# A fused scan and feed-forward kernel: another order of SyncE's transfers in its first quarter

## The chip, the cores and the metric

The kernel runs on one core of one Trainium2 chip. The metric is the device time of one execution in microseconds (us); the lower, the better. A core has four engines that compute: TensorE (PE, matrix products; its weight loads are listed apart as PEld), VectorE (DVE), ScalarE (ACT) and GpSimd (POOL). SyncE (SP) computes nothing: in this kernel it issues nearly all transfers between memory and the core's buffers (DMA), one after another, in the order of the program.

## The reference, cut to what matters

A scan (`mamba2_ssd`, 4 batches, 8 heads, 768 tokens, head size 32, state size 16) makes `x` of 3072 tokens by 256; a feed-forward block with a quick GELU follows.

```python
# scan: a is a decay per token and head, B and C are the state's input and output
log_a = np.log(np.clip(a, 1e-06, 1.0))
for c in range(nc):                            # chunks of 32 tokens
    cum = np.cumsum(la, axis=-1)
    L = np.exp(cum[:, :, :, None] - cum[:, :, None, :]) * causal
    M = np.einsum('bhin,bhjn->bhij', Cc, Bc) * L
    y_intra = np.einsum('bhij,bhjd->bhid', M, xc)
    y_inter = np.einsum('bhin,bhnd->bhid', Cc, state) * np.exp(cum)[:, :, :, None]
    y[:, :, sl] = y_intra + y_inter
    state = decay_full * state + sum_j(Bc * xc * decay_from_j)   # written short
# feed-forward: x (3072, 256), w_in (256, 2048), w_out (2048, 256)
h = x @ w_in
g = h * (1.0 / (1.0 + np.exp(-1.702 * h)))
return (g @ w_out).astype(np.float32)
```

The two weight matrices arrive as 64-bit floats and are turned into 32-bit ones on the core.

## The kernel before

The tokens are worked off in six groups of 512. A group is two pairs; a pair is 256 tokens, two chunks of 128. Pairs 0 and 1 are group 0, pairs 2 and 3 group 1, pairs 4 and 5 group 2 (the third). While TensorE computes the feed-forward part of one group, the scan of the next group's pairs is put between its matmuls.

The weights come in ten pieces, 0 to 5 of w_in and 6 to 9 of w_out. A piece is fetched as raw 64-bit words into one of four buffers of the tag "bits", and VectorE and ScalarE turn it into floats in four steps; after the last of them (`join`) the buffer is free:

```python
    def words(name):
        return wide.tile([P, 2 * PN], U32, tag="bits", name=name, bufs=BUFS)   # BUFS = 4
    # fields(i): DVE L178, L181, the first readers of a fetched piece
    # clamp(i):  ACT L189, L190      rounded(i): DVE L194
    NEXT = {1: (6,), 4: (7,), 5: (8,), 7: (9,)}

    def join(i):
        ...                            # DVE L205, L211: the piece's floats to w_in or w_out
        for n in NEXT.get(i, ()):
            fetch(n)                   # SyncE L166: the next piece into a buffer that is free

    def narrow(i):
        rounded(i)
        if i + 1 < len(PIECES):
            fields(i + 1)
        join(i)
```

The decays `a` of later pairs reach the core by a detour: `store_a` clips them (VectorE L341) and stores them to a scratch tensor in memory, and `spread` reads them back, copied to all partitions, into a buffer of the same four. `decay` scans what was spread:

```python
    def spread(p):
        if p - 2 in ra:
            ra[p] = ra[p - 2]
        else:
            ra[p] = words(f"a{p}").bitcast(FP32)...        # cut
        for i, side in enumerate(SIDES):
            nc.sync.dma_start(out=ra[p][side], in_=scratch[...])     # SyncE L237, a<-scratch

    def decay(p):
        ...
        nc.vector.tensor_tensor_scan(out=L, data0=ra[p]..., data1=idents..., ...)   # DVE L388
        for k in range(2):
            ends(p, k)                                               # DVE L437
```

`load(p)` loads b, c and x of a pair (SyncE L140; for pairs from 4 on, `load_blocks` loads B and C in another layout, SyncE L124, and `load` adds b and x). `spread_rows(b)` loads the a of a whole batch in another layout (SyncE L246, af); `clip_rows` and `decay_rows` work on it (VectorE L447, L460). `turn(p)` transposes b and c of a pair on TensorE (tp, L554), copies them out (ACT L547) and makes CsT on VectorE (L612). `gain` is TensorE's A (L657), `score` its cb (L626), `finish` its y (L730, L742); `finish` is the last reader of the pair's x.

Group 0 runs as sixteen steps of `hidden(0, f)` (TensorE h, L783) and then sixteen of `project_all(0)` (TensorE o, L900), step f of which reads w_out's block f, so four steps use one piece. At its end VectorE (L906, ob) empties the two banks of o, and the third h of group 1 takes the bank that is emptied first. Work of the other engines is hung to these steps:

```python
    at(in_hidden[0], 5, store_a)
    at(in_hidden[0], 6, lambda: pick_a(PG))
    at(in_hidden[0], 9, lambda: fan_all(PG))
    at(in_hidden[0], 9, since_fanned)
    for i, k, c in ((2, 1, 1), (3, 2, 2), (4, 4, 4), (5, 6, 6), (6, 9, 12), (7, 12, 15)):
        at(in_hidden[0], k, lambda i=i: narrow(i))
        at(in_hidden[0], c, lambda i=i: clamp(i + 1))
    at(in_hidden[0], 5, lambda: spread(PG + 1))
    at(in_hidden[0], 6, lambda: load(PG + 1))                 # PG = 2
    n, p = 2 * PG, 3 * PG
    pairs = PG, PG + 1
    at(in_project[0], 0, lambda: turn(PG), lambda: narrow(8))
    at(in_project[0], 1, lambda: clamp(9))
    at(in_project[0], 2, lambda: decay(PG + 1), lambda: clip_rows(1),
       lambda: decay_rows(1), lambda: turn(PG + 1))
    at(in_project[0], 5, lambda: narrow(9))
    at(in_project[0], 9, lambda: gain(pairs), lambda: score(pairs), lambda: keep_both(pairs),
       lambda: weigh(PG), lambda: weigh(PG + 1))
    at(in_project[0], 13, lambda: finish(pairs))
    at(in_project[0], 14, lambda: mix_in(1), lambda: mix_in(2), lambda: mix_in(3),
       lambda: turn_blocks(2), lambda: mix_y(1), lambda: decay(n))
    for k in range(PG):
        at(in_project[0], 8 + k, lambda k=k: load(2 * PG + k))
    for k, i in enumerate((9, 13)):
        at(in_project[0], i, lambda k=k: spread(2 * PG + k))
```

Each engine keeps the order of the program, SyncE too: a transfer that waits for a buffer holds up those behind it. At the start `keep_busy` lets TensorE multiply ones while the first data are on their way.

Of the kernel before, what the change touches and what calls it, by code (L numbers as in the profile page):

```python
# [16 lines left out]
P = 128  # L17
# [18 lines left out]
def kernel(  # L36
# [31 lines left out]
    nc = tc.nc  # L68
# [16 lines left out]
    PG = CG // 2  # L85
    R = 4
    Q = NH // R
    H = P // 2
# [27 lines left out]
    def load_blocks(p, queues=(nc.sync, nc.sync)):  # L116

        g, n = divmod(p, PG)
        b, c = divmod(2 * p, NC)
        for queue, name, src in zip(queues, "CB", (C, B)):  # L120
            if n == 0:
                blocks[name, g] = raw.tile([P, 2, PG * P], FP32, tag="z", name=f"z{name}{g}", bufs=2)
            for r in range(R):
                queue.dma_start(  # L124
                    out=blocks[name, g][32 * r:32 * r + 32, :, n * P:(n + 1) * P],
                    in_=src[b, Q * r:Q * r + Q, c * P:(c + 2) * P].rearrange(
                        "q (i f) n -> i q (f n)", i=32))

    def load(p, parts=None):
        if parts is None:  # L130
            parts = "bcx" if p < 2 * PG else "bx"
            if p >= 2 * PG:
                load_blocks(p)
        for part in parts:
            dst, src, e = {"b": (rb, B, N), "c": (rc, C, N), "x": (rx, x, D)}[part]
            dst[p] = raw.tile([P, 2, NH, e], FP32, tag=part, name=f"{part}{p}", bufs=3)
            for k in range(2):
                b, c = divmod(2 * p + k, NC)
                sl = slice(c * P, (c + 1) * P)
                nc.sync.dma_start(out=dst[p][:, k], in_=src[b, :, sl, :].rearrange("h s d -> s h d"))  # L140
# [9 lines left out]
    def words(name):  # L150
        return wide.tile([P, 2 * PN], U32, tag="bits", name=name, bufs=BUFS)

    def fetch(i):
        name, f, n = PIECES[i]
        if n == 2 and f % 4:
            t = pieces.pop(i - 1)[:, 2 * n * DM:]
        else:
            t = pieces[i] = words(f"bits{i}")
            t = t[:, :2 * n * DM]
        if name == "in":  # L160
            src = moe_w_in[:, 2 * f * P:2 * (f + n) * P].rearrange("(k p) e -> p k e", p=P)
            dst = t.rearrange("p (k e) -> p k e", k=NK)
        else:
            src = moe_w_out[f * P:(f + n) * P, :].rearrange("(f p) e -> p f e", p=P)
            dst = t.rearrange("p (f e) -> p f e", f=n)
        nc.sync.dma_start(out=dst, in_=src)  # L166
        t = t.rearrange("p (e w) -> p e w", w=2)
        bits[i] = t[:, :, 0], t[:, :, 1]
# [5 lines left out]
    def fields(i):  # L174
        hi, cols = bits[i][1], slice(0, PIECES[i][2] * DM)
        mantissa[i] = wide.tile([P, PN], U32, tag="m", name=f"m{i}")[:, cols]
        power[i] = wide.tile([P, PN], U32, tag="p2", name=f"p2{i}")[:, cols]
        nc.vector.tensor_scalar(out=power[i], in0=hi, scalar1=0x7FF00000, scalar2=None,  # L178
                                op0=ALU.bitwise_and)

        nc.vector.tensor_scalar(out=mantissa[i], in0=hi, scalar1=0x000FFFFF,  # L181
                                scalar2=0x00100000, op0=ALU.bitwise_and, op1=ALU.bitwise_or)

    def clamp(i):


        e = power[i]
        z = e.bitcast(FP32)
        nc.scalar.activation(z, e, AF.Relu, scale=-8.0, bias=edge[:, 0:1])  # L189
        nc.scalar.activation(e, z, AF.Relu, scale=-1.0, bias=edge[:, 1:2])  # L190
# [5 lines left out]
                                       op0=ALU.mult, op1=ALU.add)  # L196


    NEXT = {1: (6,), 4: (7,), 5: (8,), 7: (9,)}

    def join(i):

# [6 lines left out]
        else:  # L209
# [4 lines left out]
            op0=ALU.mult, op1=ALU.mult)  # L214
        for n in NEXT.get(i, ()):
            fetch(n)
# [6 lines that stand above are left out]
# [5 lines left out]
# [5 lines that stand above are left out]
            ra[p] = words(f"a{p}").bitcast(FP32)[:, :2 * NH * H].rearrange(  # L233
                "p (k e) -> p k e", k=2)
        b, c = divmod(2 * p, NC)
        for i, side in enumerate(SIDES):
            nc.sync.dma_start(  # L237
                out=ra[p][side],
                in_=scratch[c:c + 2, i, b * NH:(b + 1) * NH].rearrange("c h i -> c (h i)").unsqueeze(
                    0).to_broadcast([H, 2, NH * H]))  # L240
# [3 lines left out]
    def spread_rows(b):  # L244
        raf[b] = raw.tile([P, NC, P], FP32, tag="af", name=f"af{b}", bufs=1)
        nc.sync.dma_start(out=raf[b].rearrange("p c s -> p (c s)"),  # L246
                          in_=a[b].unsqueeze(1).to_broadcast([NH, N, S]))
# [9 lines left out]
    for r in range(R):  # L257
        (nc.sync, nc.scalar)[r % 2].dma_start(
            out=az0[32 * r:32 * r + 32].rearrange("p k s -> p (k s)"),
# [26 lines left out]
    ones = const.tile([P, P], FP32, name="ones")  # L286
# [34 lines left out]
    def fold_ident(k):  # L321
# [12 lines left out]
        out=cum.rearrange("p k s -> p (k s)"), data0=carry.rearrange("p k s -> p (k s)"),  # L334
# [13 lines left out]
    def pick_a(p):  # L348

        b, c = divmod(2 * p, NC)  # L350
        X = ffn.tile([P, 2, DM], FP32, tag="ob", name=f"X{p}")
        X = fans[p] = X.rearrange("p k (q i) -> p k q i", q=Q)
        for q in range(Q):
            nc.scalar.activation(X[:, :, q], az[:, c:c + 2], AF.Copy, scale=pick[:, b, q:q + 1])
# [5 lines left out]
        out=same, in_=same, pattern=[[-N, NH], [0, D]], compare_op=ALU.is_ge,  # L360
        fill=0.0, base=0, channel_multiplier=1)
    nc.gpsimd.affine_select(
        out=same, in_=same, pattern=[[N, NH], [0, D]], compare_op=ALU.is_ge,
# [4 lines left out]
    for t, head in ((whose[:, 1:], PG), (whose[:, :1], 1)):  # L368
# [8 lines left out]
        out=part, in_=same[:, :, 0].rearrange("p (r q) -> p q r", q=Q), op=ALU.add, axis=AX.X)  # L377
# [36 lines left out]
    def keep_busy(n):  # L414

        t = bank("busy")
        for i in range(4 * n):
            nc.tensor.matmul(out=t[:, :P], lhsT=ones, rhs=ones,
                             start=True, stop=True, skip_group_check=True)

    def decay_heads(p, r, ab):
# [116 lines left out]
    def bank(name):  # L538
        return ps.tile([P, 4 * P], FP32, tag="ff", name=name)

    def area(name):
        return psa.tile([P, R, 4 * P], FP32, tag="cb", name=name)
# [34 lines left out]
    def turn_blocks(g):  # L577

        t = {}
        for name in "CB":  # L580
            t[name] = ssd.tile([P, TG], FP32, tag=f"{name}t", name=f"{name}t{g}", bufs=1)
            nc.vector.transpose(
                out=t[name].rearrange("p (n i f) -> p n f i", n=PG, i=32),
                in_=blocks.pop((name, g)).rearrange("p h (f n) -> p f h n", n=N))
        for n in range(PG):
            s = st[g * PG + n] = {}
            s["BT"], s["tp"] = (
                t[name][:, n * 2 * P:(n + 1) * 2 * P].rearrange("p (k i) -> p k i", k=2)
                for name in "BC")
# [240 lines left out]
    def mix_y(g):  # L830
        mixed_y[g] = ffn.tile([P, 4, HT], FP32, tag="my", name=f"my{g}", bufs=1)
        mix(mixed_y[g], yT[g].rearrange("p k (t e) -> p k t e", t=2))
# [231 lines left out]
    def differ_of(p, rs):  # L1064
        differ(p, [(r, ab[p, r]) for r in rs])

    keep_busy(2)
    ab0 = area("ab0")
    for r in range(R):
        ab[0, r] = ab0[:, r, :2 * Q * H]  # L1070
# [40 lines left out]
    finish((1,))  # L1111
    join(1)
    load(PG)
    spread_rows(1)
    fields(2)
    clamp(2)
    add_up(1, (3,))
# [2 lines left out]
    def at(places, i, *work):  # L1120
        places.setdefault(i, []).extend(work)

    in_hidden = [{} for _ in range(NG)]
    in_project = [{} for _ in range(NG)]
# [2 lines left out]
        for i, side in enumerate(SIDES):  # L1127
            nc.sync.dma_start(out=scratch[:, i].rearrange("c r i -> r c i"), in_=az[:32, :, side])

    at(in_hidden[0], 5, store_a)  # L1130
    at(in_hidden[0], 6, lambda: pick_a(PG))
    at(in_hidden[0], 9, lambda: fan_all(PG))
    at(in_hidden[0], 9, since_fanned)
    for i, k, c in ((2, 1, 1), (3, 2, 2), (4, 4, 4), (5, 6, 6), (6, 9, 12), (7, 12, 15)):
        at(in_hidden[0], k, lambda i=i: narrow(i))
        at(in_hidden[0], c, lambda i=i: clamp(i + 1))
    at(in_hidden[0], 5, lambda: spread(PG + 1))
    at(in_hidden[0], 6, lambda: load(PG + 1))
    n, p = 2 * PG, 3 * PG
    pairs = PG, PG + 1  # L1140
    at(in_project[0], 0, lambda: turn(PG), lambda: narrow(8))
# [6 lines left out]
    at(in_project[0], 13, lambda: finish(pairs))  # L1148
    at(in_project[0], 14, lambda: mix_in(1), lambda: mix_in(2), lambda: mix_in(3),
       lambda: turn_blocks(2), lambda: mix_y(1), lambda: decay(n))  # L1150
    for k in range(PG):
        at(in_project[0], 8 + k, lambda k=k: load(2 * PG + k))
    for k, i in enumerate((9, 13)):
        at(in_project[0], i, lambda k=k: spread(2 * PG + k))


    after = {}
# [83 lines left out]
    k = NF // 2 - 1  # L1241
# [6 lines left out]
    for g in range(2, NG):  # L1248
        n, p = (g + 1) * PG, (g + 2) * PG
# [52 lines left out]
        k = NF // 2 - 1  # L1302
# [42 lines left out]
```

## Time and profile before

The time before is 369.91 us, the median of three runs (367.86 to 371.13). The profiled execution has a span of 366.9 us.

| engine | busy us | share of the span |
|---|---|---|
| PE | 351.3 | 96% |
| PEld | 301.7 | 82% |
| DVE | 250.9 | 68% |
| ACT | 148.0 | 40% |
| POOL | 12.9 | 4% |

The page cuts the span into 40 equal slices of 9.17 us. PE and DVE are the busy tenths of a slice, PEclk the clock that TensorE was granted in tenths of full speed, DMA the busy share of the sixteen DMA engines (an overflow shows as 0), and GB/s what they moved:

```profile
PE   7889999799699999998999999999999999999996
...
DVE  5799966994776989694869384779393355274453
...
PEclk9899999899699999999999999999999999999999
DMA  5898697405486000066101525100010000010001
```

In the first eleven slices, some 100 us, lie nearly all the slices in which TensorE is less than 0.8 busy; there the weights are fetched and turned into floats. A wait in the profile is written as who waited for whom, and the chain of waits follows the work that ended last back through the program. SyncE's rows in the timeline (SPq) are the issues, not the movement of the data.

### The profile page before, as it was taken

The page shows a single profiled execution, that of the slowest core. Times are in us where ns is not written, and L with a number is a line of the kernel's source. Part 1 is how long each engine was busy: PE and PEld are TensorE (multiplying, and loading weights), DVE is VectorE, ACT ScalarE, POOL GpSimd, SP SyncE. Part 2 cuts the span into 40 slices and gives each one's busy share as a digit, 9 for nine tenths or more (in the row PEclk, how much of TensorE's full clock was granted, in tenths as well). Part 3 has the DMA queues.
Part 4 walks back from the last instruction along what each step waited for, and adds up shares of the span by engine and source line. Part 5 has one row for each costly group of instructions (what it writes and reads, how often), then busy time and mean ns, then how long its engine had stood idle before and what let it go on. Part 6 is the DMA issues. An engine that isn't in the chain of part 4 may idle for free.

```text
span 366.9 us, 9051 instructions
## 1 busy us (share of the span) xinstructions
PE 351.3 (96%) x3880; PEld 301.7 (82%) x3880; DVE 250.9 (68%) x479; ACT 148.0 (40%) x329; POOL 12.9 (4%) x40
## 2 busy tenths in 40 slices
PE   7889999799699999998999999999999999999996
PEld 6554468687279999987999989999989999989996
DVE  5799966994776989694869384779393355274453
ACT  4588564003143431553433364333354331453330
POOL 6310000100000010000000000000000000000000
PEclk9899999899699999999999999999999999999999
DMA  5898697405486000066101525100010000010001
GB/s 120 145 364 196 186 188 178 74 2 113 119 158 107 13 2 2 25 159 127 53 3 38 92 70 98 23 2 2 1 60 4 0 2 1 2 57 2 0 2 57
DMA packets 73055, 26.10 MB, mean 71 GB/s; under 512 B 58552, under 2 KB 66616, under 8 KB 73016
## 3 DMA queue, kind: packets, MB, share of 16 engines
q1 hardware_dynamic: 72184, 25.14, 30.3%
q8 instruction: 30, 0.49, 0.6%
q10 hardware_dynamic: 832, 0.39, 0.4%
q14 instruction: 9, 0.07, 0.1%
HBM read 22.28 MB, written 3.24 MB: 70 GB/s over the span
## 4 chain that ended last, share of the span: by engine, by line
PE 75%; DMA 11%; DVE 6%; SPq 5%; issue 2%; ACT 0%; POOL 0%; DVEq 0%; POOLq 0%
PE acc L964 34%; PE X L858 18%; PE Y L868 13%; DMA bits<-in_moe_w_out_dram 4%; SPq L140 4%; DMA c<-in_C_dram 3%; PE o L900 2%; PE h L783 2%; PE y L742 2%; PE cb L626 2%; DMA a<-scratch 2%; DMA bits<-in_moe_w_in_dram 2%; PE y L730 1%; DVE L L388 1%; PE A L657 1%
## 5 line engine op out<-in xcount | busy, mean ns | idle before, releaser
L964 PEld LDWEIGHTS acc<-mw,mg 128*128 128x128 f32 x480 | 67.1, 191 | 4.0
L964 PE MATMUL acc<-mw,mg 128*128 128x128 f32 x480 | 68.9, 275 | 0.0
L863 ACT ACTIVATE ac<-X 128x256 f32<-128x256 f32 x76 | 29.1, 383 | 83.7 <-PE X L858 83.2
L983 DVE TENSOR_TENSOR gT<-Y,ac 128x512 f32<-128x512 f32 x38 | 26.2, 690 | 41.5 <-PE Y L868 36.5
L835 ACT ACTIVATE gT<-gT 128x512 f32<-128x512 f32 (+1 forms) x76 | 39.3, 519 | 32.2 <-DVE gT L983 31.7
L964 PEld LDWEIGHTS acc<-w_out,gT 128*128 128x128 f32 x320 | 44.1, 191 | 2.6
L858 PE MATMUL X<-my,mi 128*128 128x256 f32 x152 | 45.3, 381 | 0.0
L964 PE MATMUL acc<-w_out,gT 128*128 128x128 f32 x320 | 45.3, 275 | 0.0
L983 DVE TENSOR_TENSOR gT<-Y,b 128x256 f32<-128x256 f32 x38 | 15.9, 419 | 35.3 <-PE Y L868 35.3
L783 PE MATMUL h<-yT,w_in 128*128 128x512 f32 x72 | 34.7, 640 | 3.2 <-DVE ob L906 3.0
L783 PEld LDWEIGHTS h<-yT,w_in 128*128 128x128 f32 x72 | 14.5, 205 | 21.3 <-issue 15.8
L900 PE MATMUL o<-w_out,gT 128*128 128x256 f32 x128 | 28.5, 381 | 0.0
L826 DVE TENSOR_TENSOR mg<-gT 128x512 f32<-128x512 f32 x40 | 27.2, 680 | 0.0
L900 PEld LDWEIGHTS o<-w_out,gT 128*128 128x128 f32 x128 | 24.1, 190 | 3.5 <-issue 0.3
L858 PEld LDWEIGHTS X<-my,mi 128*128 128x128 f32 x152 | 24.7, 191 | 1.4
L964 PEld LDWEIGHTS acc<-mw,gT 128*128 128x128 f32 x160 | 23.1, 191 | 1.8
L964 PE MATMUL acc<-mw,gT 128*128 128x128 f32 x160 | 24.3, 276 | 0.0
L964 PE MATMUL acc<-w_out,mg 128*128 128x128 f32 x160 | 24.0, 275 | 0.0
L388 DVE TENSOR_TENSOR_SCAN L<-a,idents 128x1024 f32<-128x1024 f32 x9 | 20.5, 2283 | 4.9 <-DMA a<-scratch 4.9
L964 PEld LDWEIGHTS acc<-w_out,mg 128*128 128x128 f32 x160 | 22.8, 191 | 1.2
L858 PE MATMUL X<-yT,w_in 128*128 128x256 f32 x76 | 23.3, 391 | 0.0
L863 ACT ACTIVATE b<-X 128x256 f32<-128x256 f32 x38 | 14.6, 384 | 21.3 <-PE X L858 20.8
(143 smaller groups left out, 505.9 us busy)
## 6 DMA issues: line engine op xcount, KB each, us to landing
a<-scratch SPq DMA_DIRECT2D x18, 256.0 KB, 5.5
bits<-in_moe_w_out_dram SPq DMA_DIRECT2D x4, 1024.0 KB, 7.8
x<-in_x_dram SPq DMA_DIRECT2D x24, 128.0 KB, 3.2
out_dram<-c SPq DMA_DIRECT2D x9, 256.0 KB, 4.2
bits<-in_moe_w_in_dram SPq DMA_DIRECT2D x4, 512.0 KB, 4.9
bits<-in_moe_w_in_dram SPq DMA_DIRECT2D x2, 1024.0 KB
b<-in_B_dram SPq DMA_DIRECT2D x24, 64.0 KB, 2.8
zB<-in_B_dram SPq DMA_DIRECT2D x36, 32.0 KB, 1.9
```

The lines of the kernel that those rows point to most:

```text
L140: nc.sync.dma_start(out=dst[p][:, k], in_=src[b, :, sl, :].rearrange("h s d -> s h d"))
L388: nc.vector.tensor_tensor_scan(out=L, data0=ra[p].rearrange("p k e -> p (k e)"), data1=idents.rearrange("p h i -> p (h i)"), initial=0.0, ...
L626: nc.tensor.matmul(out=s["cb"][side, r, k].rearrange("p (q i) -> p q i", q=Q), lhsT=BT[rows, k, side], rhs=CT[rows, k, :, side], start=Tru ...
L783: nc.tensor.matmul(out=h, lhsT=w_in[:, k, f * P:(f + 1) * P], rhs=yT[g][:, k], start=(k == 0), stop=(k == NK - 1))
L826: nc.vector.tensor_tensor(out=t[:, 0:2], in0=B[:, :, 1], in1=B[:, 0], op=ALU.subtract)
L835: nc.scalar.activation(o, i, AF.Silu, scale=GELU_SCALE)
L858: nc.tensor.matmul(out=s["X"], lhsT=lhsT, rhs=rhs, start=i == "1", stop=i == "4", skip_group_check=True)
L863: nc.scalar.activation(copy, s["X"], AF.Copy)
L868: nc.tensor.matmul(out=o, lhsT=lhsT, rhs=rhs, start=s.pop("new", False), stop=i != "5", skip_group_check=True)
L900: nc.tensor.matmul(out=o[k // 2][:, k % 2], lhsT=gT[g, f // 2][:, f % 2, k * P:(k + 1) * P], rhs=w_out[:, f], start=(f == 0 and k % 2 == 0 ...
L964: nc.tensor.matmul(out=o[k] if type(o) is list else o[:, cols], lhsT=h[:, cols], rhs=w, start=(j == 0 and (i, k) in begins), stop=(j == NF ...
L983: nc.vector.tensor_tensor(out=o, in0=v, in1=w, op=ALU.add)
```

## The change

It puts SyncE's transfers of this stretch in another order, so that what can start at once does not stand behind what waits for a buffer. Pieces 7 and 8 of w_out are no longer fetched by the joins of pieces 4 and 5 but right after the stores to scratch, and piece 9 by the join of piece 5 instead of piece 7. The loads of pair 3 follow pieces 7 and 8. The spread of pair 3's a and the rows of batch 1 (af) come later, behind piece 9. The transfers of pairs 4 and 5 begin earlier, the spread of pair 4's a first, and x of pair 5, which waits for the x of pair 2 to be used up, comes last instead of standing in front of both spreads. One clamp on ScalarE moves behind an eviction of h. In `keep_busy` ten matmuls with 64 columns take the place of eight with 128.

SyncE's issues as the two programs have them, from the loads of pair 2 on (number of transfers in brackets):

| before | after |
|---|---|
| b, c, x of pair 2 (6) | b, c, x of pair 2 (6) |
| af (1) | scratch<-az (2) |
| piece 7 (1) | piece 7 (1) |
| scratch<-az (2) | piece 8 (1) |
| a of pair 3 (2) | b, c, x of pair 3 (6) |
| piece 8 (1) | piece 9 (1) |
| b, c, x of pair 3 (6) | a of pair 3 (2) |
| piece 9 (1) | af (1) |
| zC, zB, b, x of pair 4 (12) | a of pair 4 (2) |
| zC, zB, b, x of pair 5 (12) | zC, zB, b, x of pair 4 (12) |
| a of pairs 4 and 5 (4) | zC, zB, b of pair 5 (10) |
| | a of pair 5 (2) |
| | x of pair 5 (2) |

```diff
-    NEXT = {1: (6,), 4: (7,), 5: (8,), 7: (9,)}
+    NEXT = {1: (6,), 5: (9,)}
...
         t = bank("busy")
-        for i in range(4 * n):
-            nc.tensor.matmul(out=t[:, :P], lhsT=ones, rhs=ones,
+        for i in range(n):
+            nc.tensor.matmul(out=t[:, :H], lhsT=ones, rhs=ones[:, :H],
                              start=True, stop=True, skip_group_check=True)
...
-    keep_busy(2)
+    keep_busy(10)
...
     load(PG)
-    spread_rows(1)
     fields(2)
...
-    at(in_hidden[0], 5, store_a)
+    at(in_hidden[0], 5, store_a, lambda: fetch(7), lambda: fetch(8),
+       lambda: load(PG + 1))
...
-    for i, k, c in ((2, 1, 1), (3, 2, 2), (4, 4, 4), (5, 6, 6), (6, 9, 12), (7, 12, 15)):
+    for i, k, c in ((2, 1, 1), (3, 2, 2), (4, 4, 4), (5, 6, 7), (6, 9, 12), (7, 12, 15)):
...
-    at(in_hidden[0], 5, lambda: spread(PG + 1))
-    at(in_hidden[0], 6, lambda: load(PG + 1))
+    at(in_hidden[0], 9, lambda: spread(PG + 1), lambda: spread_rows(1))
...
-    for k in range(PG):
-        at(in_project[0], 8 + k, lambda k=k: load(2 * PG + k))
-    for k, i in enumerate((9, 13)):
-        at(in_project[0], i, lambda k=k: spread(2 * PG + k))
+    at(in_project[0], 6, lambda: spread(n), lambda: load(n), lambda: load_blocks(n + 1),
+       lambda: load(n + 1, "b"), lambda: spread(n + 1))
+    at(in_project[0], 9, lambda: load(n + 1, "x"))
```

## The prediction, before the changed kernel had run

> **What bounds the kernel now.** I read the page's table of engines first: TensorE (PE) is busy 351.3 of 366.9 us. So the bound is TensorE, and only its idle time and its slow clock can be won. The 40 slices say where: the row of the granted clock has one low stretch, a 6 near 92 to 101 us. Next, the waits of 60 to 140 us and of the first 60 us, because every moved transfer lies there. Columns: engine, line, releaser, us in total, times, longest.
>
> ```profile
> DVE L L388 <- DMA a<-scratch: 4.9, 1, 4.9
> ...
> PE h L783 <- DVE ob L906: 3.0, 1, 3.0
> ...
> DVE p L178 <- DMA bits<-in_moe_w_out_dram: 2.8, 1, 2.8
> ...
> PE A L657 <- DVE CsT L612: 2.4, 1, 2.4
> ```
>
> TensorE stands still twice behind VectorE (DVE), and VectorE behind a transfer both times. A third, 0.9 us, is TensorE's own wait for c of pair 3 (tp L554). I number the pieces of weights from 0; pieces 6 to 9 are w_out. The chain of waits ties the first stop to piece 9 and the second to SyncE's queue (SPq): start, length, what.
>
> ```profile
> 54.31 6.57 DMA bits<-in_moe_w_out_dram
> ...
> 70.28 0.43 DVE CsT L612
> 70.76 1.11 PE A L657 x49
> ...
> 83.12 1.24 SPq L140
> 84.47 0.59 SPq L237
> 85.10 6.42 DMA a<-scratch
> 91.61 2.30 DVE L L388
> 94.43 0.61 DVE ob L906
> 95.09 6.67 PE h L783 x8
> ```
>
> The last row leads further: 8 matmuls of h took 6.67 us, while the timeline has the 8 before them at 3.60. Stretches of 3.41 us (columns: length; busy us of PE, weight load, DVE, ACT, POOL; granted clock; DMA share; GB/s) say why:
>
> ```profile
> 66.96:70.37 3.41, 1.35 (x8) 0.78 (x6) 2.74 (x5) 0.00 (x0) 0.49 (x3) 1.00 0.24 60
> 70.37:73.78 3.41, 3.02 (x119) 2.52 (x119) 3.38 (x4) 0.00 (x0) 0.58 (x1) 0.50 0.39 39
> 90.85:94.26 3.41, 1.26 (x3) 0.20 (x2) 2.61 (x3) 0.78 (x2) 0.00 (x0) 1.00 0.75 121
> 94.26:97.67 3.41, 2.58 (x3) 1.18 (x4) 3.41 (x4) 0.00 (x0) 0.00 (x0) 0.50 0.46 161
> 97.67:101.09 3.42, 3.42 (x5) 1.35 (x4) 1.32 (x5) 0.60 (x1) 0.00 (x0) 0.50 0.26 70
> ```
>
> After each stop the clock is halved: for one stretch after the first, for two after the second. A stop costs its idle time and then the slow clock.
>
> **What the Trainium skill says.** "TensorE: Matmul & The Clock Gate", section "What's actually happening": a free-running window of 3413 ns, and half clock after an idle one. The trace agrees in the length (edges at 70.37, 73.78, 94.26, 101.09), but 1.35 us busy of 3.41 was already too little. "DMA: Bandwidth & Descriptors", section "Anatomy of one DMA — SWDGE (gpsimd) path": the engines that move data wait on no semaphore (it says so of DMA engines in general); the wait sits on the issuing sequencer. The trace agrees: the issue of x<-in_x waited 12.6 us for y L742 (till 82.71), and a<-scratch behind it started at 84.47. "Perfetto Trace Analysis", section "DMA Instruction — HWDGE (DVE, Sync)": an issue's profiled time leaves out the movement. Agrees: piece 8 took 0.55 us to issue and 7.84 to land.
>
> **The change part by part.** The order of TensorE, VectorE and GpSimd stays; ScalarE (ACT) swaps one clamp with one h eviction, which removes at most TensorE's 0.25 us wait at 40.02. So I keep all durations and recompute only waits.
>
> (a) *Transfers.* Speeds from stretches before: 48.50 to 52.20 us moved 323 GB/s, the landing of piece 8, so 1 MB takes about 3.5 us. 45.00 to 48.50 us moved 130 GB/s while both halves of a<-scratch were in flight, so that 0.5 MB takes about 4.5. b, c and x of pair 3 took 52.2 to 57.0 less gaps, about 4. Now I queue them in the new order. The stores need the clip of az (DVE L341, 34.49, with its memset done at 35.4): 35.4 to 37.3. Piece 7 is issued at 37.4, 2.1 later than before, and lands about 42.3 to 43; VectorE wants it at 44.81. Piece 8 lands about 46 (before 52.46; wanted 49.6). Then b, c, x of pair 3 by about 50 (before, c at 55.67; wanted 54.8), piece 9 by about 53.5 (before 60.9). a of pair 3 needs the buffer of piece 6, free at 48.5 when that is joined: issued about 49, landed about 58. a of pair 4 needs piece 7's, free about 53.3: landed about 63.5, instead of 91.5.
>
> (b) *VectorE.* It leaves piece 7's rounding (L194) at 49.6 us. Without the two waits of 2.86 and 2.76 us: fields of piece 8 (2 x 0.65) to 50.9, join (2 x 1.2) to 53.3, CsT of pair 2 behind ScalarE's copies about 54.9, piece 8's rounding 56.1, fields of piece 9 57.4, join 59.8. The scan of a of pair 3 (2.28) then starts at 59.8, not 64.57, and CsT L612 of pair 3, 6.1 us later by the old spacing (70.70 less 64.57), ends at 65.9.
>
> (c) *First stop.* TensorE loses the 0.9 us wait for c, so it reaches A L657 at 67.2 instead of 68.02. CsT is done at 65.9: no stop, slack 1.3. Before, the stop ended at 70.76 and A with cb ran till 73.73 at half clock, 2.97 us; the same two groups at full clock run from 101.69 to 103.59, 1.90. They now end at 69.1. The gain at this point is 73.73 less 69.1, 4.6 us: 0.9 (c), 2.7 (68.02 to 70.76), 1.0 (clock). TensorE then needs 7.1 (o), 2.4 (y), 5.3 (o) as before and starts h of group 1 at 83.9 instead of 88.5.
>
> (d) *Second stop.* VectorE: join of piece 9 69.5, states 72, two weighings 74.3, differences of w_in 78.7, transposes 80.6, my (needs yT, at 79.7) 82.2. a of pair 4 has been there for 18 us, so the scan runs at once: 84.5, ends 85.0, and ob from 85.0 to 86.3. TensorE's third h wants ob's bank after two h of 1.8 us, at 87.5. No stop, slack 1.8 for the first bank. This removes 2.97 us, and 6.67 less 3.60, 3.07, of slow clock: 6.0.
>
> (e) *Start-up matmuls.* Before, 16 passes of 128 columns took 3.78 us, 0.236 each. Now 20 passes of 64 columns: at 0.118 to 0.236 each, 2.4 to 4.7 us, an estimate from that row by columns alone or by count alone. Masks follow without a wait, and then TensorE waits till 6.80 for DVE part L376, so an earlier end moves nothing by itself. It can shift which stretch has the slow clock (now 12.35 to 15.76). I put it at 0, give or take 1.5.
>
> Sum: 4.6 + 6.0 = 10.6 us; after 115 us TensorE's order has no long gap, so I carry the sum to the end: 369.91 less 10.6 is 359.3. I add 0.7 for small waits that a new alignment brings: **360.0 us**.
>
> **The rivals.**
> 1. *The transfers are the bound of 45 to 61 us.* The DMA share is 0.9 to 1.1 in most stretches there, and one order of the same bytes cannot finish them sooner. For it: the total is unchanged. Against it: 43 to 45 us had a share of 0.10, and 61 to 63 us 0.07, and a and af, wanted late, leave the front of the queue. If piece 9 comes about 61 after all, the first stop stays with its clock, 3.7 us: 363.7.
> 2. *a of pair 3 takes the place of piece 9.* It now waits for a buffer and stands behind 1 MB. If it lands at 62 and not 58, the scan is 2.2 us later than in (b), CsT ends at 68.1, and TensorE stops 0.9 us, perhaps without losing its clock (0.86 us at 55 us cost none): 361. If the half clock comes too, 362.
> 3. *VectorE becomes the bound at ob.* Its slack is 1.8 us in (d), worked out through some 30 us of steps. If two of them slip by 1.5 each, TensorE stops 1.2 us there and may lose one stretch of clock, 1.7 us: 363.
> 4. *The clock falls elsewhere.* The gaps of the first 25 us are near what costs a stretch: 2.27 busy of 3.41 in 8.94 to 12.35 us was followed by half clock. Plus or minus 1.7.
>
> Against all of them stands that the second stop is cured by order alone: its transfer is small, and the DMA share was 0.00 from 75 to 80 us.
>
> **Range and chances.** The second stop's 6 us I hold 85% sure, the first's 4.6 about 75%. Both right: 357 to 361. One lost: about 364. 2% faster is below 362.5. Range 356.8 to 365.0. Faster by over 2%: 0.80; within 2%: 0.18; slower: 0.02.
>
> **What would show it.** Right: waits of VectorE for bits<-in_moe_w_out and a<-scratch gone or below 1 us; no wait of A L657 for CsT, nor of h L783 for ob; tp L554 no longer waits for c; granted clock 1.00 from 66 to 105 us; the 8 matmuls of h after ob in about 3.6 us; A of pairs 4 and 5 at about 91 us, not 101.69. Step (a) is wrong if piece 7 lands after 44.8, or a of pair 3 after 60. The sum is wrong if both stops are gone and yet the tail from 115 us on takes longer than 252 us: then work that was hidden has come onto the path. Wrong altogether: a new stop of over 2 us between 40 and 60 us, where the store's new place delays piece 7.

## The result and the profile after

The changed kernel took 358.06 us in the median of four runs (357.88 to 358.74), the kernel before beside it 369.11 (367.86 to 371.13): a ratio of 0.970, 95% interval 0.965 to 0.975. Measured again, as the last experiment, it was 358.47 against 366.86, ratio 0.979 (0.974 to 0.984). The medians of the changed kernel differ by 0.4 us between the two, those of the kernel before by 2.3, so the gain is 11.1 us the first time and 8.4 the second. The section on the hardware tells what the clock may have to do with it.

The table of engines of the page after has TensorE 347.5 us busy of 355.9 (98%, before 96%). Behind the third slice, none with a low share is left but the last, and none with a low clock anywhere:

```profile
PE   8789999999999999999999999999999999999996
...
PEclk9999999999999999999999999999999999999999
DMA  5898799563672000664005045000010000010001
```

A 0 in the row of DMA is a share below 0.1 and not an overflow; shares from 0.9 on show as 9.

Both stops are missing from TensorE's waits. This is that list whole, for the whole span (who waited for whom, us in total, times, longest):

```profile
PE tp L554 <- DMA b<-in_B_dram: 1.3, 1, 1.3
PE busy L418 <- DVE ones L287: 1.2, 1, 1.2
PE h L800 <- ACT yT L762: 0.8, 1, 0.8
PE y L742 <- issue: 0.7, 1, 0.7
PE A L657 <- DMA x<-in_x_dram: 0.5, 1, 0.5
PE Y L868 <- DVE gT L983: 0.3, 1, 0.3
PE cb L626 <- ACT CT L547: 0.3, 1, 0.3
```

There is no A behind CsT, no h behind ob, and no tp behind c. All that is left of over 1 us lies in the first 17 us. The chain of waits, which led through transfers and VectorE before, stays on TensorE through the whole disputed stretch (start, length, what):

```profile
55.27 12.09 PE o L900 x56
67.36 0.72 PE A L657 x47
68.08 1.14 PE cb L626 x63
69.22 7.11 PE o L900 x32
76.33 0.97 PE y L730 x56
77.30 1.42 PE y L742 x89
78.72 5.38 PE o L900 x24
84.09 6.87 PE h L783 x16
90.96 0.77 PE A L657 x53
```

The sixteen h of group 1 follow one another in 6.87 us; before, the last eight alone took 6.67. The two stretches that followed the first stop, in the columns of the prediction's table:

```profile
66.96:70.37 3.41, 3.41 (x128) 2.69 (x127) 3.38 (x8) 0.00 (x0) 0.00 (x0) 1.00 0.56 108
70.37:73.78 3.41, 3.41 (x17) 3.01 (x16) 3.27 (x8) 0.00 (x0) 0.00 (x0) 1.00 0.33 49
```

TensorE is busy for all of both and keeps the full clock.

Where the 11.0 us between the two profiled spans come from can be read off the starts of the same piece of work in the two timelines of TensorE:

| TensorE begins | before | after | difference |
|---|---|---|---|
| h of group 0, 512 columns | 24.51 | 25.19 | +0.7 |
| o behind tp of pair 3 | 55.84 | 55.11 | -0.7 |
| A of pairs 2 and 3 | 68.02, on hold till 70.76 | 67.29 | -0.7, then -3.5 |
| o behind cb | 73.73 | 69.15 | -4.6 |
| h of group 1 | 88.52 | 83.93 | -4.6 |
| A of pairs 4 and 5 | 101.69 | 90.89 | -10.8 |
| acc of group 1, first | 114.34 | 103.55 | -10.8 |
| end of the span | 366.9 | 355.9 | -11.0 |

By the end of the first stop 4.6 us are won, although h of group 0 began 0.7 us late; the second gives 6.2, and from there on nothing changes but 0.2.

### The profile page after: what moved, and what is told of

Its sections match the earlier page's. It is cut to its first block, busy times and chain, and to the rows that moved or that the text cites. A ratio compares the mean times of both kernels' runs of the same rounds, so it can differ in the third digit from the quotient of the medians.

```text
span 355.9 us, 9055 instructions
## 1 busy us (share of the span) xinstructions
PE 347.5 (98%) x3884; PEld 300.8 (85%) x3884; DVE 250.6 (70%) x479; ACT 147.5 (41%) x329; POOL 12.5 (4%) x40
## 4 chain that ended last, share of the span: by engine, by line
PE 93%; SPq 2%; DMA 2%; DVE 1%; ACT 1%; issue 0%
PE acc L964 35%; PE X L858 18%; PE Y L868 14%; PE h L783 9%; PE o L900 8%; PE y L742 2%; SPq L140 2%; PE cb L626 2%; PE y L730 2%; PE A L657 1%; DMA b<-in_B_dram 1%; PE h L800 1%; DMA az<-in_a_dram 1%; PE tp L554 0%; DVE c L987 0%
## 5 line engine op out<-in xcount | busy, mean ns | idle before, releaser
L964 PEld LDWEIGHTS acc<-mw,mg 128*128 128x128 f32 x480 | 67.2, 192 | 3.9
L783 PE MATMUL h<-yT,w_in 128*128 128x512 f32 x72 | 31.5, 594 | 0.0
L783 PEld LDWEIGHTS h<-yT,w_in 128*128 128x128 f32 x72 | 13.6, 190 | 15.9 <-issue 14.3
L868 PE MATMUL Y<-yT,mi 128*128 128x256 f32 x76 | 22.9, 383 | 0.3 <-DVE gT L983 0.3
```

The source lines that it names most:

```text
L783: nc.tensor.matmul(out=h, lhsT=w_in[:, k, f * P:(f + 1) * P], rhs=yT[g][:, k], start=(k == 0), stop=(k == NK - 1))
L868: nc.tensor.matmul(out=o, lhsT=lhsT, rhs=rhs, start=s.pop("new", False), stop=i != "5", skip_group_check=True)
L964: nc.tensor.matmul(out=o[k] if type(o) is list else o[:, cols], lhsT=h[:, cols], rhs=w, start=(j == 0 and (i, k) in begins), stop=(j == NF ...
```

## The experiments

Each run's median is told with the ratio to the kernel before that was run beside it on the same chip and its 95% interval, where that is of use. The median is of all runs; the ratio leaves out those that took over 1.5% more than the fastest of their kernel. Three chips were used, so results of different chips are compared only through that ratio. Each run has one profile.

### Each stop by itself

**x_last**: the kernel before with x of pair 5 behind the spreads.

```diff
-    for k in range(PG):
-        at(in_project[0], 8 + k, lambda k=k: load(2 * PG + k))
-    for k, i in enumerate((9, 13)):
-        at(in_project[0], i, lambda k=k: spread(2 * PG + k))
+    at(in_project[0], 8, lambda: load(n))
+    at(in_project[0], 9, lambda: load_blocks(n + 1), lambda: load(n + 1, "b"),
+       lambda: spread(n))
+    at(in_project[0], 13, lambda: spread(n + 1), lambda: load(n + 1, "x"))
```

> The kernel before with one thing changed: the load of x of pair 5 is issued behind the spreads of pairs 4 and 5 and not ahead of them. Theory (the second stop is a small transfer behind a wait for a buffer, and costs its 2.97 us and 3.07 us of halved clock): a of pair 4 lands before 80 us, h L783 does not wait for ob, the 8 matmuls of h after it take 3.6 us; 369.1 less 6.0 is about 363.1 us. Rival A (only the idle time is won, h is slow for another reason): about 366. Rival B (the stop moves to another wait at the same place, such as ob behind the rest of VectorE's work): 368 or more.

Measured: 362.24 us, ratio 0.987 (0.981 to 0.993). TensorE's timeline has the sixteen h without a gap, and of the two stops TensorE's waits have only the first, with 3.0 us:

```profile
89.79 7.03 PE L783 MATMUL h<-yT,w_in 128*128 128x512 f32 x16
96.75 0.84 PE L657 MATMUL A<-x,Be 64*32 64x64 f32 x56
```

The second stop is cured by the place of two transfers in the queue alone. Rival B, a new wait at the same place, is out; the gain by the ratio, 4.8 us (2.5 to 7.1), fits 6.0 and would fit rival A's 3 as well, so that the clock's share needed a test of its own.

**first_half**: the kernel before with the first half of the order. Start, clamp and second half stay.

```diff
-    NEXT = {1: (6,), 4: (7,), 5: (8,), 7: (9,)}
+    NEXT = {1: (6,), 5: (9,)}
-    spread_rows(1)
-    at(in_hidden[0], 5, store_a)
+    at(in_hidden[0], 5, store_a, lambda: fetch(7), lambda: fetch(8),
+       lambda: load(PG + 1))
-    at(in_hidden[0], 5, lambda: spread(PG + 1))
-    at(in_hidden[0], 6, lambda: load(PG + 1))
+    at(in_hidden[0], 9, lambda: spread(PG + 1), lambda: spread_rows(1))
```

> The kernel before with the first half of the new order alone (pieces 7 and 8 and the loads of pair 3 behind the stores to scratch, piece 9 with the join of piece 5, a of pair 3 and af behind it); the transfers of pairs 4 and 5, the clamp and the start-up matmuls stay as before. Theory: the first stop and its slow clock go, and the wait for c with them, 4.6 us, and the second stop stays whole, 6 us later in cost than in the changed kernel: about 364.5 us, with the stop of h for ob near 3 us and half clock after it. Rival (pieces 8 and 9 land no sooner, so that the gain of the first stop comes from the earlier spreads of pairs 4 and 5 or from the start-up): about 368 to 369, with the waits of VectorE for w_out still 5 us in sum.

Measured: 365.58 us, ratio 0.993 (0.989 to 0.996), so 2.7 us (1.5 to 3.9) and not 4.6. The mechanism is as expected: in its profile the first stop is gone with its waits for w_out, and the second is there:

```profile
DVE L L388 <- DMA a<-scratch: 4.6, 1, 4.6
...
PE h L783 <- DVE ob L906: 2.6, 1, 2.6
```

The rival is out, but the size was wrong. The profile shows where a part of it went: with the old start-up matmuls TensorE ran at half clock for three stretches between 14 and 25 us, the kernel before for one, so that h of group 0 began at 28.28 us instead of 24.51. TensorE reached A of pairs 2 and 3 at 70.38 us and went on at once, little sooner than in the kernel before, where the first stop ended at 70.76. The mean clock of the runs fits this: 0.987, against 0.985 before, where one half-clock stretch less would add 0.005.

**first_undone** and **second_undone** ask the same from the other side: the changed kernel without its first half, and without its second half. The edits are the two diffs above, taken back.

> The changed kernel with the first half of the order put back (af early, pieces 7 to 9 fetched by the joins of 4, 5 and 7, a of pair 3 ahead of piece 8); the transfers of pairs 4 and 5 and the start-up matmuls stay as changed. The first half alone brought 2.4 us in the median, where 4.6 were expected. Theory 1 (the first stop costs what was worked out, 2.7 to 3.6 us of idle time and 1.0 of clock, and the start's cold runs hid a part of it in the run of the first half alone): 358.1 and 4 to 4.6 make 362.1 to 362.7 us, with A L657 waiting some 3 us for CsT and half clock after it. Theory 2 (the first stop is worth only 2.4): about 360.5, with a stop that is shorter, or no half clock.

Measured: 365.62 us, ratio 0.986 (0.979 to 0.994), by the ratio the same as x_last, which has the old first half and the second stop cured as well. In the profile the waits are longer than in the kernel before, where VectorE waited 5.6 us in sum and 2.9 at most for w_out:

```profile
DVE p L178 <- DMA bits<-in_moe_w_out_dram: 7.9, 2, 5.4
```

TensorE stood 1.5 us at o for the floats of a piece and 3.8 at A for CsT. Neither theory had foreseen that the stop would grow. Apart from start and clamp, what differs from the kernel before is what is queued behind piece 9: in first_undone a of pair 4 follows it (issued at 55.29, piece 9 at 54.48), in the kernel before B and C of pair 4 do.

**undone_a4_later** puts this to the test: first_undone, with the spreads of pairs 4 and 5 behind the loads, as in x_last.

> As the run first_undone (first half of the order put back, new start), but the spreads of pairs 4 and 5 follow the loads of pairs 4 and 5, with only x of pair 5 behind them. In first_undone a of pair 4 was issued right behind piece 9 (55.3 against 54.5 us), piece 9 took 9.0 us to land, VectorE waited 5.4 us for it and the time was 365.6. Theory (a spread in flight slows the piece of weights it is queued next to, even from behind): piece 9 lands in 6.5 to 7 us as before, VectorE waits under 3.2 us for it, A for CsT about 3 us: 362 to 362.7. Rival (piece 9 was slow by chance): the same as first_undone, 365 to 366.

Measured: 362.14 us, ratio 0.988 (0.984 to 0.993). VectorE's waits for w_out are as expected:

```profile
DVE p L178 <- DMA bits<-in_moe_w_out_dram: 4.3, 2, 2.2
```

Piece 9, issued at 53.88 us, was in use at 59.97; in first_undone, issued at 54.48, at 63.62. The bytes and their order up to piece 9 are the same. Yet the theory is not shown: in six profiles with no spread queued next to it, piece 9 took 6.0 to 7.0 us to land, and in seven with one right behind it 6.3 to 9.0, among them the changed kernel with 7.2 and 6.6. So a spread behind a piece may cost it something, but the rival, chance, can account for most of these 3 us; nor do the ratios of the two runs, 0.986 and 0.988, show any difference in time. On the same chip as undone_a4_later, the changed kernel took 358.47: by this pair the first half is worth 3.7 us.

> The changed kernel with the transfers of pairs 4 and 5 put back into their old order (both loads, then both spreads); the first half of the order, the clamp and the new start-up matmuls stay. Theory (a late start is swallowed by the first stop while that is there, because VectorE and the transfers and not TensorE set its end; with the stop gone the start is on the path, so that the first half needs the new start to show its 4.6 us): 358.1 plus 6.0, about 364, with little spread from the start, and the stop of h for ob near 3 us. Rival (the first half is worth 2.4 us with any start, as in the run of it alone): about 366.

Measured: 364.21 us, ratio 0.991 (0.987 to 0.994), against 358.47 and 0.979 of the changed kernel on the same chip. By the ratios the second half is worth 4.4 us, where 6.0 were expected; the medians differ by 5.7, but they set 22 runs with a tail up to 368.1 us against six. The profile is of a run of 366.58 us, longer than the median:

```profile
DVE L L388 <- DMA a<-scratch: 6.1, 1, 6.1
...
PE h L783 <- DVE ob L906: 5.3, 1, 5.3
...
DVE p L178 <- DMA bits<-in_moe_w_out_dram: 1.9, 1, 1.9
```

The stop was 5.3 us there, not 3. TensorE began h of group 1 at 84.95 us, 3.6 sooner than in the kernel before, but a of pair 4 was in use only 1.2 us sooner (90.36 for 91.61): what the first half had won was in part waited away at the second stop. Piece 9 came 1.9 us late, with the same first half that has no such wait in the changed kernel. The reason that the theory gave, that the first half needs the new start, is not shown by this run: first_half and second_undone differ only by start and clamp, and their gains over the kernel before, 2.7 us (1.5 to 3.9) and 3.5 (2.3 to 4.7), overlap.

### The clock by itself

**warm_stop**: the kernel before; TensorE multiplies ones in its second stop. No transfer is moved.

```diff
+    def keep_warm(n):
+        t = area("warm")
+        for i in range(n):
+            nc.tensor.matmul(out=t[:, 0, :P], lhsT=ones, rhs=ones,
+                             start=True, stop=True, skip_group_check=True)
             hidden(1, 2 * int(step[1:]) + i)
+        if step == "H0":
+            keep_warm(12)
```

> The kernel before, with 12 matmuls of ones (24 passes of 128 columns, at full clock some 0.11 us each, 2.6 us) put on TensorE between the second and the third h of group 1, where it stands still for 2.97 us; no transfer is moved. Theory (the slow h comes from the clock, which falls because TensorE idles): the stop remains in the sense that the third h still starts when ob is done, near 95 us, but the granted clock stays at 1.00 and the 8 matmuls of h take 3.6 us instead of 6.67: about 3.1 us less, 366.0 us. Rival (h is slow because of transfers or of VectorE's reads at that time, and the clock only happens to be low): no gain, 369 us or somewhat more.

Measured: 372.62 us, ratio 1.013 (1.005 to 1.020): about 1% slower, against the expectation. At the disputed place it did what the theory said. TensorE's timeline there, and the stretch of the last eight h, with the clock in the third column from the end:

```profile
92.09 2.84 PE L425 MATMUL warm<-ones 128*128 128x128 f32 x24
95.65 3.70 PE L790 MATMUL h<-yT,w_in 128*128 128x512 f32 x8 [0.72 <-DVE ob L913]
99.28 0.84 PE L664 MATMUL A<-x,Be 64*32 64x64 f32 x56
```

```profile
95.65:99.28 3.63, 3.63 (x8) 1.44 (x8) 3.60 (x6) 0.60 (x1) 0.00 (x0) 1.00 0.53 173
```

The third h still starts when ob is done, 0.56 us later than before. Yet the eight h take 3.70 us, not 6.67, and A begins 2.4 us sooner than in the kernel before. So the slow h was the clock, and the clock fell because TensorE idled. In the profiled run, the slowest of the six with 376.18 us, time was lost later, in five gaps of 1.26 to 1.97 us in which TensorE waited for nothing that the profile shows, 8.2 us in sum; the kernel before has one, of 1.28.

**warm_bf16** fills the stop with half as many instructions.

```diff
-            nc.tensor.matmul(out=t[:, 0, :P], lhsT=ones, rhs=ones,
+            nc.tensor.matmul(out=t[:, 0], lhsT=identb,
+                             rhs=below.unsqueeze(1).to_broadcast([P, 8, H]),
                              start=True, stop=True, skip_group_check=True)
```

> The kernel before, with TensorE kept at work in the second stop by 12 matmuls of 512 columns in bf16 (12 passes in place of the 24 of the run warm_stop; at full clock about 0.21 us each, 2.6 us). warm_stop kept the clock at 1.00 there and had the 8 matmuls of h at 3.70 us instead of 6.67, but five later gaps on TensorE with nothing waited for, 8.2 us in sum against 1.3 before, made it slower in all. Theory (those gaps come from how many instructions TensorE's stream has and where they fall, not from the clock): with half the added instructions the gaps sit elsewhere, and the time is 368.0 less 3.1 and less or plus what gaps there are; near 365 if there are as few as before. Rival (keeping TensorE busy there causes the later gaps): slow again, 371 or more.

Measured: 369.26 us, ratio 1.001 (0.999 to 1.004). The eight h took 3.70 us once more, and A began at 99.41. Of the unexplained gaps two were left ("issue" stands for nothing waited for that the profile shows):

```profile
PE y L750 <- issue: 1.2, 1, 1.2
PE Y L876 <- issue: 0.9, 1, 0.9
```

So, by one profile of each, keeping TensorE busy does not by itself bring gaps of that size: two ways of doing it have 8.2 and 2.1 us of them. That they come from the number of instructions fits but is not shown. And neither run won anything in the end, where 3.1 us were expected: the mechanism is confirmed at its place, its worth for the whole program is not, by these runs.

### The place of piece 9

**a_before_nine**: the changed kernel with a of pair 3 ahead of piece 9.

```diff
-    NEXT = {1: (6,), 5: (9,)}
+    NEXT = {1: (6,), 6: (9,)}
-    at(in_hidden[0], 9, lambda: spread(PG + 1), lambda: spread_rows(1))
+    at(in_hidden[0], 6, lambda: spread(PG + 1))
+    at(in_hidden[0], 9, lambda: spread_rows(1))
```

> The changed kernel with a of pair 3 ahead of piece 9: it takes the buffer of piece 5, and piece 9 is fetched by the join of piece 6 into that one's buffer. Theory (the first stop is cured by piece 8 coming early, and the schedule has a slack of 1.3 to 1.7 us): piece 9 is issued near 49.5 us instead of 48.7 and lands behind a, near 57 to 58 instead of 53.5; VectorE waits about 1 to 1.5 us for it, CsT L612 of pair 3 ends about 67, and TensorE's wait at A stays under 0.5 us: 358 to 359 us. Rival (the order of piece 9 ahead of a is what cures it): piece 9 lands at 60 us or later, TensorE stops for over 2 us at A: 361 or more.

Measured: 366.06 us, ratio 0.988 (0.985 to 0.992). The rival is right. VectorE's timeline:

```profile
54.63 1.22 DVE L194 SCALAR_TENSOR_TENSOR m<-bits,m 128x1024 f32<-128x1024 uint32 x1
62.34 0.70 DVE L178 TENSOR_SCALAR p<-bits 128x1024 uint32<-128x1024 uint32 x1 [6.49 <-DMA bits<-in_moe_w_out_dram]
```

Piece 9 was issued at 48.80 us, 0.06 later than in the changed kernel, and took 13.4 us to land. In the changed kernel it stood ahead of the spread, took 7.2, and VectorE used it at 56.30 without a wait. TensorE stopped 3.8 us at A, and 1.0 at o. So the early pieces 7 and 8 alone do not cure the first stop.

### The start

**old_start** is the changed kernel with the start-up matmuls of the kernel before, **new_start** the kernel before with those of the changed one, **busy_eight** the changed kernel with `keep_busy(8)` for `keep_busy(10)`.

```diff
-        for i in range(n):
-            nc.tensor.matmul(out=t[:, :H], lhsT=ones, rhs=ones[:, :H],
+        for i in range(4 * n):
+            nc.tensor.matmul(out=t[:, :P], lhsT=ones, rhs=ones,
-    keep_busy(10)
+    keep_busy(2)
```

> The changed kernel with the start-up matmuls of the kernel before (8 of 128 columns for 10 of 64). Before, 16 passes took 3.78 us; after, 20 passes of half the columns took 4.53, so a pass costs 0.23 us whatever its columns, and the masks start 0.75 us later. Theory 1 (the start is on the path, and the new start-up matmuls cost it): the first h of 512 columns starts at 24.5 instead of 25.2 us, and the time falls by up to 0.7 us, to about 357.4. Theory 2 (the longer start-up keeps the clock up, and the cold stretch of 12.35 to 15.76 us returns without it): the start is the same within 0.4 us or worse, 358 to 359.5.

> The kernel before with the new start-up matmuls alone (10 of 64 columns for 8 of 128); no transfer is moved. The changed kernel with the old ones took 359.8 in the median, against 358.1, and spread over 3.7 us, its profile with half clock from 14.3 to 24.7 us; the changed kernel spread over 0.9. Theory (the start is a part of the gain: TensorE is kept busy till 5.5 us, the clock stays up through the waits for x and b, and a cold start no longer comes in some runs): about 1.5 to 2 us less than before, 366 to 366.5, and the first h of 512 columns at about 25.2 us with no half clock before it. Rival (the start only shifts the phase of the clock's windows, and the gain of 1.7 is chance): within 0.5 us of before.

> The changed kernel with 8 start-up matmuls of 64 columns for 10 (16 passes of 0.23 us, which end near 4.8 us instead of 5.5). Theory (passes cost by count; TensorE then waits for DVE part L376 till 6.8 as in the kernel before, and the first differ starts 0.36 us sooner, but the clock may fall at the gap before b at 15 us): like the run old_start, which had 16 passes too: 359 to 360, with half clock between 14 and 25 us in some runs. Rival (the columns count for the clock, or the shorter start wins its 0.4 us): 357.7, with no half clock.

Measured: old_start 359.8 us (357.15 to 360.89), ratio 0.979 (0.971 to 0.986); new_start 368.81, ratio 1.000 (0.998 to 1.003); busy_eight 358.24 (357.06 to 359.64), ratio 0.978 (0.973 to 0.982). In its profile old_start had TensorE at about half clock for 11 us, and h of 512 columns began at 28.37 us instead of 25.19. The stretch in old_start:

```profile
14.00:25.00 11.00, 9.18 (x166) 6.05 (x166) 5.98 (x13) 5.64 (x11) 1.91 (x3) 0.53 0.96 285
```

and in the changed kernel:

```profile
14.00:25.00 11.00, 8.56 (x198) 6.17 (x199) 9.22 (x22) 7.27 (x15) 1.91 (x3) 1.00 1.02 290
```

Such a start costs over 3 us when it comes. The clock before 25 us goes with the columns of the start-up matmuls in every profile: the six with 128 columns (before, x_last, first_half, warm_stop, warm_bf16, old_start) have one to three half-clock stretches between 12 and 25 us, the eight with 64 have none. busy_eight is one of the eight; it has as many passes as the old start, and its mean clock was 1.00 in all six runs, so that its rival, the columns, is right about the clock. None of old_start's four runs reached 1.00 (0.986 to 0.995). What this is worth in time is not settled: new_start had a higher mean clock than the kernel before (0.989 against 0.982) and yet brought nothing, which fits that a late start is waited away at the first stop; and old_start's ratio equals that of changed_again, but not the 0.970 of the first measurement. No version was clearly better than the changed kernel.

**changed_again**, the changed kernel beside the last three:

> The changed kernel once more, beside the three others on the same chip: 358.1 us, within 0.5, with no half clock up to 110 us, and a spread of about 1 us. If it spreads over 3 us like the others, its small spread was luck and the start still has cold runs.

Measured: 358.47 us, ratio 0.979 (0.974 to 0.984), from 356.82 to 360.8. The small spread of its first four runs was luck in part; three of these six have a mean clock of 0.990 to 0.995.

## Why the prediction was right

The predicted time was 360.0 us, the bare sum 359.3, and the median came to 358.06 and 358.47. The predicted gain, 9.9 us (10.6 bare), lies between the 11.1 and the 8.4 measured, so that the number alone says little about the single terms. The profile of the changed kernel follows the working step by step:

| step of the prediction | predicted us | measured us |
|---|---|---|
| (a) VectorE waits for a piece of w_out | none | none |
| (a) piece 9 lands | about 53.5 | 55.9 |
| (a) a of pair 3 lands | about 58 | 58.7 |
| (b) VectorE takes up piece 9, no wait | 56.1 | 56.30 |
| (b) scan of a of pair 3, no wait | 59.8 | 59.92 |
| (b) end of CsT of pair 3 | 65.9 | 66.05 |
| (c) TensorE reaches A of pairs 2 and 3 | 67.2, no stop | 67.29, no stop |
| (c) A and cb done | 69.1 | 69.15 |
| (c) h of group 1 begins | 83.9 | 83.93 |
| (d) ob begins | 85.0 | 84.68 |
| A of pairs 4 and 5 | about 91 | 90.89 |

What held was to keep every duration, to recompute only the waits in program order, and to count the slow clock after a stop as a part of what the stop costs. The runs then show how far each term may be trusted:

- **Step (d), 6.0 us:** right for the pair of profiles (6.2), and too large for the runs: 4.4 by the ratios of second_undone and changed_again, and 4.8 (2.5 to 7.1) by x_last. That its clock share is real, and caused by idling, is shown at its place by warm_stop and warm_bf16.
- **Step (c), 4.6 us:** right for the pair of profiles, and too large for the medians: 3.7 us by undone_a4_later against changed_again, 2.7 (1.5 to 3.9) by first_half. On the last chip the two halves, 3.7 and 4.4, make up about the whole, 7.9 by the ratio, so that the sum of 10.6 was too large there in both terms. The term that was mis-sized is the fixed sum of idle time and clock: it was taken from one execution, and both the length of a stop (2.6 us at h in first_half, 5.3 in second_undone) and the mean clock differ between executions.
- **Step (e), 0 give or take 1.5:** a pass costs by count and not by columns: 20 passes took 4.53 us, 0.227 each, the upper end of the estimate. The masks began 0.75 us later (5.53 for 4.78), and h of 512 columns 0.7. That TensorE still reached A on time is a piece of luck: 0.3 of it came back by 40 us and 0.2 more than worked out at tp. The worth of the whole step stays open.
- **Rival 1** (the transfers are the bound in any order) fell: pieces 7 to 9 all came in time, piece 9 by 0.4 us. **Rival 2** (a of pair 3 is late behind piece 9) did not come about. Its mirror image does when the two are swapped: piece 9 then takes 13.4 us to land, and TensorE stops 3.8 us at A, where the rival had 0.9. **Rival 3** (VectorE at ob) did not come about either, with ob 0.3 us ahead of plan. **Rival 4** (the clock falls elsewhere) fits the spread of the runs, as the last section shows.

One assumption was wrong without doing harm, and that was luck: that transfers of one queue can be added up one behind the other. By that sum piece 9 lands at 53.5 us, 2.6 ahead of need. It landed at 55.9, 7.2 us after its issue at 48.74; of the three times in this line of the changed kernel's trace, for pieces 7 to 9, it is the middle one:

```profile
DMA to landing us min/median/max: 6.6/7.2/8.4
```

That was 0.4 us before VectorE took it up. In second_undone, with the same order up to there, it came 1.9 us too late, and TensorE waited 0.5 us for CsT. In a_before_nine the same kind of sum (landed near 57 to 58) missed by over 4 us (62.2).

## What to carry to other kernels

Look in the issuing queue for what is ready but stands behind a transfer that waits for a buffer; moving x of pair 5 behind two spreads was a change of no bytes and no instruction, worth about 5 us of 368 in x_last. Price a stop of TensorE of over 2 us at its idle time and the half-clock stretch or stretches behind it: in these profiles each of the twelve such stops at A or h was followed by one or two. And when such a saving is sized from one profile, look at the mean clock of several runs first: it is not the same in each.

## What the runs showed of the hardware

**The mean clock of a run counts its half-clock stretches.** A stretch of 3.41 us at half clock does the work of 1.7 us, 0.0047 of a span of 362; the mean clocks come near 1.000, 0.995, 0.991, 0.986, 0.981 and 0.976. In changed_again, three runs with a clock of 1.000 took 356.8 to 357.6 us, two with 0.995 359.3 and 359.6, one with 0.990 360.8. In second_undone, of the runs behind its ratio, four with 0.999 or 1.000 took 359.9 to 361.0 us, three with 0.995 362.8 to 363.4, and five with 0.990 or 0.991 362.7 to 364.9. So one and the same program lost no clock in some runs and one or two stretches in others. The clock is not all of it: the step from 1.000 to 0.995 is some 2 to 2.6 us, more than the 1.7 of one stretch. On the last chip the mean clock was 0.984 before and 0.997 after; 0.013 of 362 is 4.7 us of a difference in means of 7.9. By this estimate up to some 60% of the gain is clock, less as far as TensorE had no work in the slow stretches. Not all of that belongs to the two stops: of the four half-clock stretches in the profile of the kernel before, one lies at the start (12.35 to 15.76 us).

**A spread between other transfers went with slow landings.** In the kernel before, the DMA engines moved 130 GB/s from 45.0 to 48.5 us, while a spread was in flight, and 323 from 48.5 to 52.2, while piece 8 landed. Piece 9 took 6.0 to 7.0 us to land with no spread next to it, 6.3 to 9.0 with one right behind it, and 13.4 in a_before_nine, with one in front and another behind. The last is one profile, and the runs don't show why.

**A start-up pass costs the same with 64 as with 128 columns**, 0.227 against 0.236 us. The 24 passes of 128 columns in warm_stop, at 92 us, took half of that, 0.118 each, so the start-up passes are slow although the granted clock of the first 3.41 us is given as 1.00.

**TensorE has gaps with nothing to wait for**, of 0.4 to 2 us each. The profiles of the kernels before and after have one each, warm_stop, with 24 passes more, has five. The cause stays open.
